# Loading q and k two tokens to a partition, with 64-column transposes, all loads on one queue and a new plan of steps

## The chip, the cores and the metric

The kernel runs on one core of a Trainium2 chip. The metric is the device time of one execution in microseconds (us), and the span of a profile is the part of it from the first to the last instruction. Engines are named as in the profile: PE is TensorE, PEld its weight loads (they overlap PE), DVE is VectorE, ACT is ScalarE, POOL is GpSimd, SP is SyncE. "L476" is a line of the kernel in question, so the same operation has other line numbers in other kernels.

## The reference

It is attention inside chunks of 64 tokens, followed by a layer that mixes tokens and then channels:

```python
# q, k, v: (8 batches, 8 heads, 576 tokens, 64), float32; nine chunks of 64 tokens
scores = (q_c @ k_c.T) / sqrt(64)             # inside each chunk
x = softmax(scores) @ v_c                     # laid out as (8, 576, 512)
theta = x @ w_theta                           # 512 x 512
y = w_tok_r @ (x * cos(theta)) + w_tok_i @ (x * sin(theta))   # 576 x 576, over tokens
u = x + y
out = u + relu(u @ w_ch)                      # 512 x 512, float32
```

## The kernel before

The batches go in four pairs. A pair has 9 blocks of 128 tokens, taken in five groups of two blocks or one (`GROUPS`); the groups of the pair's first half come first (`B0 = [0, 2, 1]`), those of its second half later (`B1 = [3, 4]`). The steps of a group are: a1 transposes q and k (`ps_qkT`), a2 makes the scores (`ps_sT`) and ACT their exponentials (`eT`), a3 multiplies by v (`ps_x`), a4 transposes x (`ps_xT`), and a5 multiplies by theta (`ps_theta`), with cosine and sine on ACT. After them come the token mixing (`ps_y`, with both token weights transposed once at the start into `wT`) and the channel step (`ps_uw`). A small planner, `Order`, keeps estimated clocks of PE, DVE and ACT and decides when the program is built in which order the steps stand. All PSUM results share four slots of 4 KB per partition.

```python
def load_qk(p, j):                       # one block of 128 tokens, one token per partition
    t = nat.tile([P, 2, H, D], FP16, name="qk16")
    nats[p, j] = t
    for ti, ap in enumerate((q, k)):
        for pp, bb, s0, n in in_ranges(j):
            nc.gpsimd.dma_start(t[pp : pp + n, ti],
                ap[2 * p + bb, :, s0 : s0 + n, :].rearrange("h s d -> s h d"))

def a1(p, g):                            # 8 full-size transposes a block, one copy
    ...
                nc.tensor.transpose(psv[:, w, e, jj * P : jj * P + P],
                    t[:, w, 2 * e : 2 * e + 2, :].rearrange("s h d -> s (h d)"), id16)
    ...
    nc.vector.tensor_copy(out=qkT[:, :, :, 0 : n * P], in_=psv[:, :, :, 0 : n * P])

def a2(p, g):                            # 64x64 array tiles, four at a time
    ...
                        nc.tensor.matmul(psv[kh * CH : kh * CH + CH, par, i, e, :],
                            qkT[par * D : par * D + D, 1, e, c0 : c0 + CH],
                            qkT[par * D : par * D + D, 0, e, c0 : c0 + CH])

# the start: weights and the first v as float32 on the hardware queue (SP), cast on chip
tok32 = [load_tok_w(0, moe_w_tok_r), load_tok_w(1, moe_w_tok_i)]
v32 = {0: load_v32(0, 0)}
wth32 = load_w32(moe_w_theta)
new_pair(0)
load_qk(0, 0)                            # q, k: software queue (POOL)
...
# each pair: main steps, and filler steps put between them
od.segment(y0, (front(p, B1) if p == 0 else []) + back(p, B1), tail=3.0)
...
od.segment(mid, fill, tail=4.0)          # mid: y1 and ps_uw by turns; fill: the next pair
# ... (casts, estimates of landing times and the other steps left out)
```

The softmax here doesn't subtract the row's maximum and nothing guards it: scores larger than these inputs give would overflow.

## Time and profile before

| | before |
|---|---|
| time, median of 3 | 243.7 us (242.69 to 245.37) |
| span of the profiled run | 242.2 us |
| first transpose of q | 12.36 us |
| first `ps_y` | 53.14 us |
| from there to the end | 189.1 us |

The prediction below shows the lines of this profile and reads them. One more view belongs here. It cuts the run in two where `ps_y` first starts; its columns are the stretch, its length, then PE, PEld, DVE, ACT and POOL busy (with instructions), the granted clock, the DMA share and GB/s.

```profile
0.00:53.10 53.10, 26.92 (x354) 17.25 (x354) 17.29 (x33) 21.39 (x27) 36.38 (x51) 0.97 1.71 185
53.10:242.20 189.10, 174.11 (x2304) 119.61 (x2288) 113.89 (x188) 91.94 (x112) 71.14 (x93) 0.99 0.97 103
```

PE is empty for 26.2 of the first 53.1 us, and for only 15.0 of the 189.1 after them.

One more row of the page matters later. It gives the clock granted to PE, in tenths, in 40 slices of 6.06 us:

```profile
PEclk9999999889999999999999979999999999999999
```

The 7 is a stretch at half the clock, recorded from 138.82 to 142.24 us: eight `ps_theta` take 3.04 us there and 1.89 us at 98.12. It costs PE some 1.7 us, half of its 3.42. The first seven 9s are not a grant: the trace has no clock record before 43.25 us, and the page prints full clock where there is no record. All 61 full-size matmuls that follow one another without a gap before 43.25 us are spaced for half rate (107 ns for 128 columns).

### The profile page before, as it was taken

To read this page: it belongs to the slowest core of one execution; us is meant where nothing else is said; L and a number is where in the kernel's file an instruction comes from. 1 tells how busy PE (TensorE), PEld (TensorE's weight loads), DVE (VectorE), ACT (ScalarE), POOL (GpSimd) and SP (SyncE) were. 2 spreads that over 40 slices of the span, in tenths; PEclk is the share of its full clock that TensorE was granted. 3 is DMA by queue.
4 is the path that set the end of the run, shared out by engine and by line. 5 is a ranking of instruction groups with operands and counts; after the bars stand their busy time and mean duration, and the time that the engine had idled before them with its cause. 6 is when DMAs were issued, how large, how long until landed. Compare 5 with 4: busy or idle time off the path is not lost.

```text
span 242.2 us, 6094 instructions
## 1 busy us (share of the span) xinstructions
PE 201.0 (83%) x2642; PEld 136.9 (57%) x2642; DVE 131.2 (54%) x220; ACT 113.3 (47%) x138; POOL 107.5 (44%) x143
## 2 busy tenths in 40 slices
PE   0036767589999879999998799999997999998992
PEld 0014554257766756567777555676775556765751
DVE  0103482546546764784567617763866387635453
ACT  2205526662664528823835266536333865361132
POOL 8444776999920019896800097987200100000000
PEclk9999999889999999999999979999999999999999
DMA  6999999999990119999991199999911115100226
GB/s 220 267 194 217 155 157 170 140 132 137 140 80 4 46 46 113 191 226 195 131 62 46 46 106 169 179 232 152 82 46 46 46 56 184 46 0 3 87 96 207
DMA packets 120953, 29.38 MB, mean 121 GB/s; under 512 B 113632, under 2 KB 114656, under 8 KB 120928
## 3 DMA queue, kind: packets, MB, share of 16 engines
q0 software_dynamic: 108048, 14.03, 91.4%
q1 hardware_dynamic: 12880, 14.98, 21.3%
q8 instruction: 20, 0.33, 0.6%
q14 instruction: 5, 0.04, 0.1%
HBM read 33.06 MB, written 9.44 MB: 175 GB/s over the span
## 4 chain that ended last, share of the span: by engine, by line
PE 60%; DVE 5%; ACT 4%; issue 2%; DVEq 0%
PE ps_y L477 25%; PE ps_uw L497 13%; PE ps_theta L421 10%; PE ps_qkT L314 5%; PE ps_uw L504 3%; PE ps_xT L392 2%; DVE uT L485 2%; ACT xT L399 2%; ACT eT L343 1%; PE ps_sT L336 1%; ACT relu L510 1%; DVE x L378 1%; DVE qkT L321 1%; DVE z L444 1%; ACT sin L435 0%
## 5 line engine op out<-in xcount | busy, mean ns | idle before, releaser
L477 PE MATMUL ps_y<-wT,z 128*128 128x288 f16 x512 | 68.5, 286 | 5.5 <-ACT eT L343 2.1
L477 PEld LDWEIGHTS <-z 128*128 128x128 f16 x512 | 48.9, 98 | 19.6 <-issue 3.4
L485 DVE TENSOR_TENSOR uT<-ps_y,xT 128x576 f16<-128x576 f32 x32 | 24.2, 757 | 37.5 <-PE ps_y L477 37.5
L497 PE MATMUL ps_uw<-wch,uT 128*128 128x512 f16 x144 | 41.7, 383 | 1.5 <-ACT xT L399 1.5
L217 POOL DMA_DIRECT2D qk<-in_q_dram x40 | 35.8, 902 | 11.2 <-DMA qk<-in_q_dram 6.9
L236 POOL DMA_DIRECT2D v<-in_v_dram x48 | 36.8, 815 | 7.2 <-DMA qk<-in_k_dram 3.9
L217 POOL DMA_DIRECT2D qk<-in_k_dram x40 | 36.1, 909 | 4.1 <-DMA qk<-in_k_dram 3.0
L314 PE MATMUL ps_qkT<-id,qk 128*128 128x128 f16 x288 | 21.4, 231 | 19.9 <-DMA qk<-in_q_dram 14.5
L421 PE MATMUL ps_theta<-wtheta,xT 128*128 128x512 f16 x128 | 34.0, 418 | 3.7 <-ACT xT L399 3.7
L321 DVE COPY qkT<-ps_qkT 128x2048 f16<-128x2048 f16 (+1 forms) x20 | 21.7, 1114 | 26.0 <-PE ps_qkT L314 26.0
L510 ACT ACTIVATE relu<-ps_uw 128x512 f32<-128x512 f32 x36 | 21.2, 600 | 28.4 <-PE ps_uw L504 28.2
L431 ACT ACTIVATE cos<-ps_theta,pihalf 128x1024 f16<-128x1024 f32 (+1 forms) x20 | 20.6, 1029 | 23.9 <-PE ps_theta L421 21.9
L504 PE MATMUL ps_uw<-id,uT 128*128 128x128 f16 x144 | 31.8, 221 | 0.0
L399 ACT COPY xT<-ps_xT 128x1024 f16<-128x1024 f16 x16 | 15.9, 1015 | 32.1 <-PE ps_xT L392 32.1
L314 PEld LDWEIGHTS <-qk 128*128 128x128 f16 x288 | 17.8, 103 | 22.6 <-DMA qk<-in_q_dram 14.5
L516 DVE TENSOR_TENSOR o<-ps_uw,relu 128x512 f32<-128x512 f32 x36 | 24.1, 688 | 11.0 <-ACT relu L510 10.8
L405 POOL COPY xT<-xTm 128x256 f16<-128x256 f16 x8 | 3.0, 402 | 59.7 <-ACT xTm L403 59.7
L378 DVE TENSOR_TENSOR x<-ps_x,recip 128x512 f16<-128x512 f32 x36 | 24.9, 692 | 1.2
L343 ACT ACTIVATE eT<-ps_sT 128x1024 f16<-128x1024 f32 (+1 forms) x20 | 18.3, 937 | 15.1 <-PE ps_sT L336 15.1
L421 PEld LDWEIGHTS <-xT 128*128 128x128 f16 x128 | 13.1, 106 | 20.3 <-issue 5.1
L497 PEld LDWEIGHTS <-uT 128*128 128x128 f16 x144 | 14.1, 98 | 15.4 <-issue 0.3
L444 DVE TENSOR_TENSOR z<-x,cos 128x1024 f16<-128x1024 f16 x16 | 11.0, 688 | 20.1 <-ACT cos L431 20.0
(41 smaller groups left out, 179.3 us busy)
## 6 DMA issues: line engine op xcount, KB each, us to landing
out_dram<-o SPq DMA_DIRECT2D x32, 256.0 KB, 2.3
qk<-in_q_dram POOLq DMA_DIRECT2D x32, 128.0 KB, 6.0
qk<-in_k_dram POOLq DMA_DIRECT2D x32, 128.0 KB, 6.2
v<-in_v_dram POOLq DMA_DIRECT2D x34, 64.0 KB, 5.5
v<-in_v_dram POOLq DMA_DIRECT2D x14, 128.0 KB, 5.8
wtok<-in_moe_w_tok_r_dram SPq DMA_DIRECT2D x1, 1152.0 KB, 6.0
wtok<-in_moe_w_tok_i_dram SPq DMA_DIRECT2D x1, 1152.0 KB, 10.0
w<-in_moe_w_theta_dram SPq DMA_DIRECT2D x1, 1024.0 KB, 12.9
```

The source lines that it names most:

```text
L217: nc.gpsimd.dma_start(t[pp : pp + n, ti], ap[2 * p + bb, :, s0 : s0 + n, :].rearrange("h s d -> s h d"),)
L236: nc.gpsimd.dma_start(v16[pp : pp + m, sl, :, 0:D], v[2 * p + bb, :, s0 : s0 + m, :].rearrange("h s d -> s h d"),)
L314: nc.tensor.transpose(psv[:, w, e, jj * P : jj * P + P], t[:, w, 2 * e : 2 * e + 2, :].rearrange("s h d -> s (h d)"), id16,)
L321: nc.vector.tensor_copy(out=qkT[:, :, :, 0 : n * P], in_=psv[:, :, :, 0 : n * P])
L378: nc.vector.tensor_tensor(out=xo, in0=px[:, :, :, 0:D], in1=recip.broadcast_to((P, 2, NE, D)), op=ALU.mult,)
L421: nc.tensor.matmul(ps[:, jj * DM : jj * DM + DM], xt[:, db, :], wtheta16[:, db, :], start=(db == 0), stop=(db == NDB - 1),)
L477: nc.tensor.matmul(psv[:, hf, 0:HS], z[:, db * P : db * P + P], wT[:, kt, hf * HS : hf * HS + HS], start=(kt == 0), stop=(kt == 2 * KT),)
L485: nc.vector.tensor_tensor(out=s["uT"][:, db, sl].rearrange("p (f c) -> p f c", f=2), in0=psv[:, :, 0:HS], in1=s["xT"][:, db, sl].rearrange ...
L497: nc.tensor.matmul(ps[:, 0:DM], uT[:, db, j * P : j * P + P], wch16[:, db, :], start=(db == 0), stop=(db == NDB - 1),)
L504: nc.tensor.matmul(ps[:, DM + db * P : DM + db * P + P], uT[:, db, j * P : j * P + P], id16,)
L510: nc.scalar.activation(out=r, in_=ps[:, 0:DM], func=AF.Relu)
L516: nc.vector.tensor_tensor(out=o, in0=ps[:, DM : 2 * DM], in1=r, op=ALU.add)
```

## The change

The intent: with two neighbouring tokens on one partition a run of q or k in memory is 512 B and not 256 B, so q and k need half as many packets. Heads must still come out as 64 rows of features each, so a transpose now takes 64 columns (one head, one token of the two), and two of them fill the array side by side. The q and k copies are split between DVE and ACT, and the k copy puts the tokens back in order. All loads go through the software queue, in the order in which they are used, cast on the way. The planner is changed as well: filler is paced by its heaviest engine, and two `ps_uw` of a pair move into the first stage of the next.

```diff
-    def load_qk(p, j):
-        t = nat.tile([P, 2, H, D], FP16, name="qk16")
+    def load_qk(p, g):
+        j0, n = GROUPS[g]
+        t = nat.tile([P, 2, H, 2, D], FP16, name="qk16")
 ...
-                    t[pp : pp + n, ti],
-                    ap[2 * p + bb, :, s0 : s0 + n, :].rearrange("h s d -> s h d"),
+                    t[(pp // 2) : (pp // 2) + m // 2, ti].rearrange(
+                        "p h t d -> p h (t d)"
+                    ),
+                    src.rearrange("h (p t) d -> p h (t d)", t=2),
 ...  a1
+        for w in range(2):
+            for e in range(NE):
+                for tk in range(2):
+                    for par in range(2):
+                        nc.tensor.transpose(
+                            psv[par * D : par * D + D, w, e, tk, 0:rows],
+                            t[0:rows, w, 2 * e + par, tk, :],
+                            id16[0:rows, 0:rows],
+                        )
+        qT = qkp.tile([P, NE, 2, P], FP16, name="qT")
+        kT = qkp.tile([P, NE, P, 2], FP16, name="kT")
-        nc.vector.tensor_copy(
-            out=qkT[:, :, :, 0 : n * P], in_=psv[:, :, :, 0 : n * P]
+        nc.vector.tensor_copy(out=qT[:, :, :, 0:rows], in_=psv[:, 0, :, :, 0:rows])
+        nc.scalar.copy(
+            out=kT[:, :, 0:rows, :].rearrange("p e s t -> p e t s"),
+            in_=psv[:, 1, :, :, 0:rows],
         )
 ...  a2
+        kT = kT.rearrange("p e s t -> p e (s t)")
+        qT = qT.rearrange("p e t s -> p e s t")
-                            qkT[par * D : par * D + D, 1, e, c0 : c0 + CH],
-                            qkT[par * D : par * D + D, 0, e, c0 : c0 + CH],
+                            kT[par * D : par * D + D, e, c0 : c0 + CH],
+                            qT[par * D : par * D + D, e, c0 // 2 : (c0 + CH) // 2, :],
 ...  the start
-    tok32 = [load_tok_w(0, moe_w_tok_r), load_tok_w(1, moe_w_tok_i)]
-    v32 = {0: load_v32(0, 0)}
-    wth32 = load_w32(moe_w_theta)
     new_pair(0)
-    load_qk(0, 0)
+    load_qk(0, B0[0])
     make_identity(nc, id16)
+    for g in B0[1:]:
+        load_qk(0, g)
+    for g in B0:
+        load_v(0, g)
+    load_w(moe_w_theta, wtheta16)
+    load_tok_w(0, moe_w_tok_r)
+    load_tok_w(1, moe_w_tok_i)
     load_batch(0, B1)
     load_w(moe_w_ch, wch16)
-    (the casts of the float32 weights and of the first v)
 ...  the plan
-        od.segment(y0, (front(p, B1) if p == 0 else []) + back(p, B1), tail=3.0)
+        main = y0[:3] + held[:1] + y0[3:] + held[1:] + ws[0:2]
+        od.segment(main, (front(p, B1) if p == 0 else []) + back(p, B1), tail=4.0)
 ...
+        main = y1[:3] + ws[2:3] + y1[3:] + ws[3:]
+        held = []
+        if more:
+            held = main[-2:]
+            main = main[:-2]
 ...  (planner: pace by the heaviest engine, copies of a step counted side by side)
```

## The prediction

> **What bounds the kernel now.** I read the page's counts first, then its slices, then the table of ten-microsecond stretches, and then the timeline of the stretches that looked wrong.
>
> ```profile
> PE 201.0 (83%) x2642; PEld 136.9 (57%) x2642; DVE 131.2 (54%) x220; ACT 113.3 (47%) x138; POOL 107.5 (44%) x143
> ...
> PE   0036767589999879999998799999997999998992
> ...
> q0 software_dynamic: 108048, 14.03, 91.4%
> ```
>
> TensorE is busy for 201.0 us of 242.2, so 41 us are empty. The PE row says where: the first eight or nine slices (6 us each), a dip at each change of batch pair, and the end. The software DMA queue takes 91.4% of the engines' time, but that share is summed over the run and says nothing yet of who waits. The stretches show it (columns after the length: PE, weight loads, DVE, ACT, POOL busy us and instructions; granted clock; DMA share; GB/s):
>
> ```profile
> 10.00:20.00 10.00, 2.90 (x21) 1.90 (x21) 0.43 (x1) 0.00 (x0) 3.48 (x4) 1.00 1.51 227
> 20.00:30.00 10.00, 7.16 (x96) 5.15 (x96) 4.09 (x8) 6.40 (x9) 6.11 (x9) 1.00 1.98 160
> ...
> 110.00:120.00 10.00, 10.00 (x92) 7.19 (x91) 4.14 (x7) 6.84 (x7) 6.96 (x9) 1.00 2.13 157
> ...
> 180.00:190.00 10.00, 7.87 (x196) 5.45 (x194) 7.17 (x14) 3.99 (x6) 0.74 (x2) 1.00 0.08 28
> ```
>
> From 10 to 20 us the PE works 2.90 us, with ACT and DVE idle as well: all wait for data. From 110 to 120 it is full while the DMA share is 2.13, so in the middle loads are hidden behind TensorE. From 180 to 190 it loses 2.13 us with no DMA to speak of (0.08): there it waits for copies and exponentials at the change of pair. In the sum over ten-microsecond rows, PE is busy 24.25 us of the first 50: 25.75 of the 41 lost us lie there.
>
> The timeline of the start names the waits:
>
> ```profile
> 12.36 0.61 PE L314 MATMUL ps_qkT<-id,qk 128*128 128x128 f16 x4 [12.36 <-DMA qk<-in_q_dram]
> 12.60 0.89 POOL L217 DMA_DIRECT2D qk<-in_q_dram  x1 [4.10 <-DMA qk<-in_q_dram]
> 14.37 0.61 PE L314 MATMUL ps_qkT<-id,qk 128*128 128x128 f16 x4 [1.40 <-DMA qk<-in_k_dram]
> ...
> 32.54 0.83 PE L280 MATMUL ps_wT<-id,wnat 128*64 128x128 f16 x10
> ...
> 39.61 3.60 PE L421 MATMUL ps_theta<-wtheta,xT 128*128 128x512 f16 x8 [0.68 <-ACT xT L399]
> ...
> 53.14 0.66 PE L477 MATMUL ps_y<-wT,z 128*128 128x288 f16 x4
> ```
>
> The first q tile, issued at 1.24 us, lands at 12.36; each following load of 1024 packets lands about 2.1 us after the last, and POOL itself waits (4.10 us): eight loads are out, and the ninth issue reuses the first one's semaphore. The token mixing, the large stage, starts only at 53.14. From there to the end are 189.1 us in which PE hardly stops. So two questions matter: when does ps_y start, and does what follows get longer?
>
> **What the Trainium skill says.** "DMA: Bandwidth & Descriptors", section Specifications, gives 512 B as the smallest transfer at line rate. The packets agree in direction: in the trace a software packet that reads 256 B and writes 128 B holds its engine 32 ns, one that reads 2048 B and writes 1024 B 98 ns, so eight times the bytes for three times the time. The same page, "Queues, rings and completion order", says that an engine takes turns between queues packet by packet. This fits the start: the float32 weights go by the hardware queue in packets of 2304 and 2048 B at 106 and 88 ns, and each 32 ns packet of q waits behind them.
>
> "TensorE: Matmul & The Clock Gate", Part 1, has the array at half rate when little used, and warns that clock records are unreliable. Both show here: eight ps_theta matmuls take 3.60 us at 39.61 and 1.89 us at 98.12, start to start 427 against 216 ns[...]. The tile transposes at 32.54 are in that half-rate time.
>
> "TensorEngine Tiling (Array Packing)", Key Properties, says that tiles load and multiply in parallel and that a change of mode drains the array; its Restrictions say that column tiling loses fast weight load. The transposes of 128x64 at 32.54, just the form that the change uses, start in pairs 3 to 6 ns apart, a pair every 107 ns. Half rate makes 128 columns 107 ns, so a pair costs one full-size transpose and its weight loads stay hidden. The drain shows as well: 125 ns from the last 64x64 matmul to the next full-size one, against 32 ns for a set of four.
>
> **The change, part by part.**
>
> Loads. For q and k two tokens make one run: 512 B read and 256 B written, so 73,728 packets become 36,864. Between the two measured sizes I estimate 41 ns each; the 108,048 packets hold v (32 ns) unchanged. POOL issues 12 loads of q and k per pair, not 20; at 0.9 us for 1024 packets this saves some 8 us of POOL per pair, hidden after the start. What counts is the order: q and k of the first three groups (2.62 MB read), their v (1.31), theta (1.05), then the two token weights (2.65), with no hardware queue beside them. In stretches of 4 us, the start of the kernel before reads at most some 340 GB/s in large packets, and in 256 B packets about 1,100 per us (282 GB/s). With 330 for q and k, 282 for v and 340 for the weights: 7.9 + 4.7 + 3.1 + 7.8 = 23.5 us. Data begins at about 2.6 us (issue at 1.24 and one 1 us issue), and I add 2 us to landing: first q about 6 us, theta about 20, last token weight about 28. The second batch of groups follows until about 38.
>
> Start of ps_y. The nine wT transposes finish last. Five of them need the second token weight; before, a group of this sort took some 0.75 us at half rate, so 3.5 us: ps_y starts at about 31.5 instead of 53.14. Theta and z for the first three groups fit between 20 and 31. Gain: 21.6 us.
>
> Casts. Thirteen casts of v, wnat and wtheta (9.8 us of ACT and DVE together) go; they lie in the waiting time and are worth nothing more than the earlier start.
>
> Work moved behind ps_y. Before, both a1 steps of the second batch and one a2 were done by 53.14 (1.95 and 0.45 us); now they come during ps_y: +2.2 us.
>
> Transposes. A group had 16 of 56 ns (0.89 us); now 16 pairs of about 58 ns (0.93). With one more mode change of about 0.11 us this is +0.15 us a group, 17 groups after the start: +2.5 us. It is on the path, as PE bounds there.
>
> Evacuation. DVE loses a copy of 1221 ns for one of 684 (the 1024-element form), 2.5 us per pair; ACT gains five k copies of about 1015 or 592 ns, 4.7 us per pair. The step gets shorter, 1.22 to about 1.0 us, as both run together. ACT was busy about 26 us per pair of 49, so it can carry this on average.
>
> Order. The last two ps_uw steps of a pair move into the next pair's first stage, the first two into that same stage, and the filler is paced by its heaviest engine, not by PE alone. PE loses 6.25, 5.34 and 3.86 us in gaps over 0.12 us in the three middle periods (half-clock stretches included), most at the change of pair. I give the new order about 1.2 us of each: -3.5.
>
> Sum: -21.6 + 2.2 + 2.5 - 3.5 = -20.4 us; 243.7 - 20.4 = 223.3, say 223 us.
>
> **The rivals.** First, column tiles that expose their weight loads: 64 columns without fast load, 107 ns for a pair at full clock too, would add 0.8 us a group, 14 us over 17 groups: 237 us. The page's restriction speaks for it; the half-rate reading of 32.54 and the 64x64 sets at 32 ns speak against it.
>
> Second, the queue does not get faster. If one queue with at most eight loads out reads at the 212 GB/s of the stretch from 12 to 16 us, 7.63 MB take 36 us, and ps_y begins at about 44: 235 us. Against it: the stretches from 24 to 44 us read 261 to 341 GB/s, and POOL needs only some 16 us to issue it all.
>
> Third, ACT becomes the bound at the change of pair. The y1 stage (second half of a pair, first batch of the next) holds five k copies, five exponentials, five relus, copies, sines and two table loads, by my sum 22.7 us of ACT in about 27 us of PE. If each a1 to a2 step now waits in ACT's queue, 2 to 3 us a pair are lost instead of 1.2 gained: 234 us.
>
> Fourth, the start is better than I think: loads overlap fully, ps_y at 26 us, and the new order removes most gaps: 213 us.
>
> **Range and chances.** The central term, the start of ps_y, I trust to 4 us; the later periods to 2 us each in sum 5. That gives 214 to 232. For less than 2% gain two rivals would have to come true together. Faster by over 2%: 0.95; within 2%: 0.04; slower: 0.01.
>
> **What would show it.** The first transposes at 6 to 8 us, not 12.4; the software queue's share near 70%; ps_y starting at 29 to 34 us; pairs of 128x64 transposes 56 to 60 ns apart at full clock (107 would be rival one); periods of ps_y 47 to 50 us long; in the stretches at the change of pair more than 7.9 of 10 us PE busy, with no new wait for the k copy. A ps_y start after 38 us, or periods longer than 51 us, would make the prediction wrong.

## The result, and the profile after

The changed kernel took 230.23 us (median of 4, 228.72 to 231.85) against 243.19 us (median of 4) for the kernel before in the same rounds. All ratios here are the mean time of one kernel's fast runs over that of the other's from the same rounds, so they are not quite the ratios of the medians: 0.9454, with a 95% interval of 0.9364 to 0.9544. Two later calls of the unchanged kernel gave 0.9582 and 0.9567, so the gain is 4 to 5.5%. The time lies inside the predicted range of 214 to 232 us, 7 us above the predicted 223.

The page of the profiled run (span 226.9 us; this run was the fastest of the four) has these lines for the ones shown of before:

```profile
PE 201.7 (89%) x2994; PEld 140.3 (62%) x2994; DVE 120.2 (53%) x214; ACT 130.5 (58%) x151; POOL 88.5 (39%) x124
...
PE   0678979997898998999898998999898998999992
...
q0 software_dynamic: 77664, 16.54, 82.3%
```

PE's busy time is the same as before, and the span is 15.3 us shorter, so its idle time fell from 41.2 to 25.2 us. The slices at the left, 0036767 before, are now 0678979. The software queue holds 30,384 packets fewer, but its share is only nine points lower, as the weights now come through it. The same ten-microsecond stretches:

```profile
10.00:20.00 10.00, 7.47 (x206) 5.99 (x206) 4.38 (x11) 6.52 (x8) 9.42 (x14) 1.00 1.81 168
20.00:30.00 10.00, 8.76 (x56) 4.79 (x55) 4.29 (x9) 8.02 (x10) 4.49 (x6) 1.00 1.53 186
...
110.00:120.00 10.00, 9.07 (x234) 7.40 (x228) 4.45 (x8) 8.82 (x9) 0.00 (x0) 1.00 0.03 11
180.00:190.00 10.00, 9.21 (x92) 5.33 (x89) 8.03 (x15) 5.75 (x9) 1.02 (x2) 1.00 0.33 96
```

From 10 to 20 us PE now works 7.47 us and not 2.90. The later rows fall in other parts of the work than before, since everything is earlier, so they cannot be compared line by line; the row from 110 is now the change of pair, with ACT busy for 8.82 us of ten. Cut at the first `ps_y`, the run reads:

```profile
0.00:33.50 33.50, 22.24 (x379) 15.62 (x379) 12.27 (x27) 18.70 (x22) 25.57 (x41) 1.00 1.52 156
33.50:226.90 193.40, 179.51 (x2620) 124.70 (x2616) 107.94 (x187) 111.82 (x129) 62.97 (x84) 0.99 0.86 112
```

The first part is 19.6 us shorter. The second is 4.3 us longer: PE is busy 5.4 us more in it and idle 1.1 us less. So in these two profiles the gain is all at the start, and a part is paid back in PE's own work. The timeline of the start:

```profile
5.79 1.07 PE L307 MATMUL ps_qkT<-id,qk 128*64 128x128 f16 x16 [5.79 <-DMA qk<-in_q_dram]
7.47 2.08 PE L307 MATMUL ps_qkT<-id,qk 128*64 128x128 f16 x48 [0.61 <-DMA qk<-in_k_dram]
...
21.38 2.85 PE L420 MATMUL ps_theta<-wtheta,xT 128*128 128x512 f16 x8
27.68 0.87 POOL L225 DMA_DIRECT2D qk<-in_k_dram  x1 [0.93 <-DMA wnat<-in_moe_w_tok_i_dram]
29.34 1.59 PE L271 MATMUL ps_wT<-id,wnat 128*128 128x128 f16 x15 [0.63 <-ACT sin L434]
33.50 2.13 PE L476 MATMUL ps_y<-wT,z 128*128 128x288 f16 x16
```

The first q is there at 5.79 us. POOL's wait at 27.68 ends with the landing of the last token weight. From there `ps_y` is 5.8 us away. The transposes of that weight run at full rate here, but they wait for a PSUM slot that ACT frees late (its sines, at 29.34) and for one that a DVE copy frees (at 31.54), and the last copy of it ends at 33.23. The sines are late in part because the theta step before them ran in part at half rate: eight `ps_theta` at 21.38 take 2.85 us, where 1.9 is the time at full rate. A second profile of the same kernel has 3.48 us for those eight, a recorded half clock from 31.61 us on, and the first `ps_y` at 35.85. This part of the start scatters from run to run.

The step that turns transposes into scores changed most in the middle of the run. In the kernel before, for a group of two blocks:

```profile
122.44 0.45 PE L336 MATMUL ps_sT<-qkT 64*64 64x64 f16 x32
122.81 1.07 PE L314 MATMUL ps_qkT<-id,qk 128*128 128x128 f16 x16
123.92 1.23 DVE L321 COPY qkT<-ps_qkT 128x2048 f16<-128x2048 f16 x1 [0.55 <-PE ps_qkT L314]
```

and in the changed kernel:

```profile
105.05 1.08 PE L307 MATMUL ps_qkT<-id,qk 128*64 128x128 f16 x32
106.39 0.68 DVE L316 COPY qT<-ps_qkT 128x1024 f16<-128x1024 f16 x1
107.11 1.30 ACT L317 COPY kT<-ps_qkT 128x1024 f16<-128x1024 f16 x1 [1.35 <-DVE qT L316]
...
112.80 2.12 PE L476 MATMUL ps_y<-wT,z 128*128 128x288 f16 x16 [0.84 <-ACT eT L342]
...
120.12 0.69 PE L335 MATMUL ps_sT<-qT,kT 64*64 64x64 f16 x32
```

The number after the start is the busy time of the instructions merged in the line. Thirty-two 64-column transposes take what sixteen full-size ones took (1.08 and 1.07 us). The same 32 score matmuls take 0.69 us and not 0.45. The two copies stand one after the other: ACT waits for DVE although they read different halves of the PSUM tile, so the step lasts 0.68 + 1.30 = 1.98 us and not 1.23. And at 112.80 `ps_y` waits for an exponential, which stands on ACT behind a k copy (109.67) and a table load of 1.28 us (110.43). Such a wait is longer here, but not new: in the same period the kernel before has one of 0.69 us at 132.52, and old_layout, below, one of 0.41 us at 120.53.

### The profile page after: what moved, and what is told of

Read it like the earlier page. It is cut to its first block, busy times and chain, and to the rows that moved or that the text cites. A ratio compares the mean times of both kernels' runs of the same rounds, so it can differ in the third digit from the quotient of the medians.

```text
span 226.9 us, 6743 instructions
## 1 busy us (share of the span) xinstructions
PE 201.7 (89%) x2994; PEld 140.3 (62%) x2994; DVE 120.2 (53%) x214; ACT 130.5 (58%) x151; POOL 88.5 (39%) x124
## 3 DMA queue, kind: packets, MB, share of 16 engines
q0 software_dynamic: 77664, 16.54, 82.3%
## 4 chain that ended last, share of the span: by engine, by line
PE 75%; ACT 14%; DVE 6%; DMA 2%; issue 1%; POOL 0%; DVEq 0%; ACTq 0%; POOLq 0%
PE ps_y L476 32%; PE ps_uw L496 13%; PE ps_theta L420 13%; ACT eT L342 5%; PE ps_qkT L307 5%; PE ps_sT L335 3%; PE ps_uw L503 3%; DMA qk<-in_k_dram 2%; PE ps_xT L391 2%; DVE uT L484 2%; DVE x L377 2%; ACT kT L317 2%; ACT cos L430 2%; ACT xT L398 2%; PE ps_x L363 2%
## 5 line engine op out<-in xcount | busy, mean ns | idle before, releaser
L246 POOL DMA_DIRECT2D v<-in_v_dram x56 | 42.1, 776 | 14.6 <-DMA qk<-in_k_dram 9.2
L496 PE MATMUL ps_uw<-wch,uT 128*128 128x512 f16 x144 | 41.0, 379 | 2.3 <-ACT xT L398 1.7
L317 ACT COPY kT<-ps_qkT 128x1024 f16<-128x1024 f16 (+1 forms) x20 | 23.4, 1193 | 17.9 <-DVE qT L316 17.9
L404 POOL COPY xT<-xTm 128x256 f16<-128x256 f16 x8 | 4.9, 652 | 72.3 <-ACT xTm L402 72.3
L420 PE MATMUL ps_theta<-wtheta,xT 128*128 128x512 f16 x128 | 31.2, 388 | 1.7 <-ACT xT L398 1.7
L307 PE MATMUL ps_qkT<-id,qk 128*64 128x128 f16 (+1 forms) x640 | 22.1, 227 | 6.4 <-DMA qk<-in_q_dram 5.8
L307 PEld LDWEIGHTS <-qk 128*64 128x64 f16 (+1 forms) x640 | 18.9, 118 | 9.4 <-DMA qk<-in_q_dram 6.2
L316 DVE COPY qT<-ps_qkT 128x1024 f16<-128x1024 f16 (+1 forms) x20 | 12.6, 636 | 22.7 <-PE ps_qkT L307 22.7
L420 PEld LDWEIGHTS <-xT 128*128 128x128 f16 x128 | 12.6, 100 | 15.7 <-ACT xT L398 2.1
L443 DVE TENSOR_TENSOR z<-x,cos 128x1024 f16<-128x1024 f16 x16 | 11.1, 691 | 20.6 <-ACT cos L430 20.4
L225 POOL DMA_DIRECT2D qk<-in_k_dram x24 | 19.2, 804 | 3.6 <-DMA wch<-in_moe_w_ch_dram 1.6
```

The source lines that it names most:

```text
L246: nc.gpsimd.dma_start(v16[pp : pp + m, sl, :, 0:D], v[2 * p + bb, :, s0 : s0 + m, :].rearrange("h s d -> s h d"),)
L307: nc.tensor.transpose(psv[par * D : par * D + D, w, e, tk, 0:rows], t[0:rows, w, 2 * e + par, tk, :], id16[0:rows, 0:rows],)
L317: nc.scalar.copy(out=kT[:, :, 0:rows, :].rearrange("p e s t -> p e t s"), in_=psv[:, 1, :, :, 0:rows],)
L420: nc.tensor.matmul(ps[:, jj * DM : jj * DM + DM], xt[:, db, :], wtheta16[:, db, :], start=(db == 0), stop=(db == NDB - 1),)
L496: nc.tensor.matmul(ps[:, 0:DM], uT[:, db, j * P : j * P + P], wch16[:, db, :], start=(db == 0), stop=(db == NDB - 1),)
```

## The experiments

Twelve kernels ran; all gave the right result. A period is the time from the first `ps_y` of a pair to that of the next, and the table shows the second one (the first holds most of the scatter of the start). The kernel before took 243.25, 243.01 and 242.17 us in the three calls. Its second period holds the stretch of half clock shown above; its third, which has none, is 48.67 us, so 48.67 is the fairer number to hold against the others: the change's period is 1.9 us longer, and those of old_layout and order_only are the same. The starts and periods are those of one profile each.

| run | median us | ratio to before, 95% | first `ps_y` | second period |
|---|---|---|---|---|
| before | | 1 | 53.14 | 50.36 |
| the change | 230.23 | 0.9454 (0.9364 to 0.9544) | 33.50 | 50.54 |
| **call 1, 3 rounds** | | | | |
| old_layout | 230.76 | 0.9491 (0.9437 to 0.9545) | 38.26 | 48.63 |
| hw_weights | 244.95 | 1.0050 (0.9997 to 1.0103) | 50.29 | 50.55 |
| old_order | 239.81 | 0.9870 (0.9825 to 0.9916) | 36.05 | 51.33 |
| order_only | 242.06 | 0.9952 (0.9902 to 1.0003) | 54.37 | 48.64 |
| **call 2, 5 rounds** | | | | |
| after_again | 232.26 | 0.9582 (0.9523 to 0.9641) | slow profile | slow profile |
| copies_together | 232.23 | 0.9594 (0.9536 to 0.9653) | 33.90 | 50.82 |
| q_interleaved | 233.40 | 0.9643 (0.9602 to 0.9684) | 36.98 | 50.40 |
| q_inter_together | 232.04 | 0.9586 (0.9548 to 0.9624) | 37.26 | 50.98 |
| **call 3, 5 rounds** | | | | |
| after_third | 230.94 | 0.9567 (0.9512 to 0.9622) | 35.85 | 50.54 |
| hybrid | 228.09 | 0.9442 (0.9393 to 0.9490) | 34.04 | 48.87 |
| hybrid_ws | 227.07 | 0.9390 (0.9357 to 0.9424) | 36.94 | 48.08 |
| weights_first | 240.79 | 0.9965 (0.9927 to 1.0002) | 45.74 | 50.54 |

### Which part brings the gain: old_layout, hw_weights, old_order, order_only

My theory was that the gain comes from the early start, that the start comes from the order of the loads on one queue, and that the two-token layout adds little. The rivals were that the layout itself, with its fewer packets, or the new plan brings it.

**old_layout** is the changed kernel with the loads, transposes and the single copy of q and k as before:

```diff
 # against the changed kernel
+    def load_qk1(p, j): ...             # one token per partition, 256 B runs, as before
+    def load_qk(p, g): for j in its blocks: load_qk1(p, j)
 # a1: 8 full-size transposes a block, one DVE copy; a2 reads qkT: as before
```

> The changed kernel with one token per partition again (128x128 transposes, one 1.22 us copy on VectorE, contiguous q), while the single queue in order of use and the new plan of steps stay. Theory (the order of the loads makes the gain, the two-token layout costs after the start): q and k packets fall back to 256 B, ps_y starts 1 to 4 us later than 33.5 (34.5 to 37.5), a set of four score matmuls goes back from 62 to 32 ns, the k copy no longer queues behind the q copy, so the periods shrink from 50.6 to 48 to 49.5; time 226 to 230, not slower than the changed kernel. Rival (the halved packets make the gain): ps_y starts at 40 us or later, time 236 or more.

It took 230.76 us, which can't be told from the change; the first `ps_y` came at 38.26 us. Both lie just above what I expected (226 to 230, and 34.5 to 37.5). These two lines of its timeline name the landing of the last token weight and the first `ps_y`:

```profile
30.72 0.88 POOL L245 DMA_DIRECT2D v<-in_v_dram  x1 [2.28 <-DMA wnat<-in_moe_w_tok_i_dram]
...
38.26 2.13 PE L467 MATMUL ps_y<-wT,z 128*128 128x288 f16 x8
```

The weight lands 3.0 us later than in the change (3.7 later than in its second profile), so the larger packets do help the start. But each later period is 1.9 us shorter than the change's, and that gives the start's gain back. As a whole the layout is worth nothing here.

**hw_weights** puts float32 weights and the first v back on the hardware queue, with their casts:

```diff
 # against the changed kernel
-        nc.gpsimd.dma_start(wnat[ri]..., ...)     # theta and the first v likewise
+        f32 = pairp.tile([P, KT + 1, S], FP32, name="wtok32", tag="uT")
+        nc.sync.dma_start(f32..., ...)            # and the casts of before
```

> The changed kernel with the float32 weights and the first v on the hardware queue and cast on VectorE and ScalarE again, two-token layout kept. Theory (order makes the gain): the first q lands at 9 to 12 us instead of 5.8, ps_y starts at 42 to 50 us, time 238 to 246. Rival (halved packets make the gain, order does not matter): ps_y before 38 us, time 234 or less.

At 244.95 us the whole gain is gone. The start of its timeline shows why:

```profile
13.09 1.06 PE L326 MATMUL ps_qkT<-id,qk 128*64 128x128 f16 x16 [13.09 <-DMA qk<-in_q_dram]
```

The first q lands at 13.09 us, although its load is issued first on its own queue and has the large packets; the first `ps_y` starts at 50.29 us. Both are a little past what I expected (9 to 12, and 42 to 50). The packets of the trace show two parts in the delay of q. Its first packet starts at 5.94 us here (5.83 in the kernel before) and at 2.96 in the change, though the load is issued at 1.24 us in all three. From 7.2 to 10 us the two queues then take turns, 369 packets of q and k to 354 of the weights (381 to 380 in the kernel before). What holds the first packet back for 3 us no run shows. The larger packets alone, next to a second queue, bring 4.1 us of start against order_only (54.37), and the longer periods take them back.

**old_order** is the change with the plan of before:

```diff
 # against the changed kernel
-        work = sum(s.load for s in filler)
+        work = sum(s.pe for s in filler)
-        main = y0[:3] + held[:1] + y0[3:] + held[1:] + ws[0:2]
-        od.segment(main, ...)
+        od.segment(y0, ...)
+        mid: y1 and ps_uw by turns, nothing held over        # and the old clock in Order.do
```

> The changed kernel with the plan of steps of the kernel before (sequence of ps_y and ps_uw, pacing by TensorE alone, copies planned one after the other). Theory (the new plan gains little): ps_y starts within 1 us of 33.5 and what follows takes 192 to 196 us instead of 193.4, time 228 to 233. Rival (the plan is what keeps ScalarE's new work off the path): what follows takes 198 us or more, time 235 or more.

This one went against me: 239.81 us. The start is early (36.05), but the first period takes 62.48 us where the change has 53.22. With an early start the second batch of the first pair comes in the first `ps_y` stage, and that stage had only four `ps_y` steps to cover it. The two lines of old_order are an ACT table load, a part of the delay, and the wait of PE:

```profile
52.08 1.28 ACT L429 ACT_TABLE_LOAD   x1 [3.53 <-PE ps_theta L419]
...
56.35 3.47 PE L419 MATMUL ps_theta<-wtheta,xT 128*128 128x512 f16 x8 [3.91 <-ACT xT L397]
```

In the changed kernel the same wait is

```profile
52.34 1.90 PE L420 MATMUL ps_theta<-wtheta,xT 128*128 128x512 f16 x8 [1.74 <-ACT xT L398]
```

because two `ps_uw` steps stand in front of it. PE in old_order waits 3.91 us for the copy of x (behind the table load, a cosine and a sine), and then the eight matmuls run at half rate, 3.47 us and not 1.90. These two items are 3.7 us of the 9.3. A second stretch of half clock, from 76.63 to 80.04 us, adds some 1.7; the rest is spread over the period and I have not followed it.

**order_only** is the other side of that: the kernel before with the new plan alone.

```diff
 # against the kernel before
-        work = sum(s.pe for s in filler)
+        work = sum(s.load for s in filler)
-        od.segment(y0, ...)
+        main = y0[:3] + held[:1] + y0[3:] + held[1:] + ws[0:2]
+        od.segment(main, ...)
+        main = y1[:3] + ws[2:3] + y1[3:] + ws[3:]    # its last two held for the next pair
 # the loads, the casts, a1 and a2 stay as before (the identity is made one block's loads later)
```

> The new plan of steps alone: loads, casts and one-token layout of the kernel before. Theory: ps_y starts near 53 us as before, the periods lose 1 us each at most; time 240 to 244 against 243.2. Rival (the plan is worth several us by itself, and the layout ate it): time 238 or less.

It took 242.06 us, 1.2 us under the kernel before, and its interval reaches 1. So the plan is worth about one microsecond with the old loads. Its second period is 1.7 us shorter than that of the kernel before, as long as the stretch of half clock costs there, and its third is the same (48.63 and 48.67). With the early loads the plan is worth 7 to 10: the ratio of 0.987 without it against 0.945 to 0.958 for the change, times 243. The two parts interact: here the plan is the condition for keeping what the loads bring. As old_order has the two-token layout too, and no run has the early loads with the old layout and the old plan, the share of the layout in this is not separated; the first period of old_order is 9.3 us longer than the change's, the later ones 0.8.

### What makes a period longer: after_again, copies_together, q_interleaved, q_inter_together

The two-token layout costs 1.9 us a period. I had two suspects from the traces: the k copy, which follows the q copy and delays an exponential (0.84 us of idle PE before the `ps_y` at 112.80 in the record, 1.03 us measured from start to start), and the score matmuls, which read q in steps of two tokens.

**after_again** is the changed kernel once more, as a base.

> The changed kernel unedited, as the measure for the other runs of this call: 0.9454 of the kernel before, within 0.009; periods 50.5 to 50.6 us.

Its profiled execution fell in the slow state (271.13 us at a granted clock of 0.77), so only its timed fast runs count: 230.22 to 233.23 us. Their ratio of 0.9582 lies above the 0.9544 that I had allowed, so the size of the gain itself differs between calls.

**copies_together** gives q and k a PSUM tile each, so that the two copies have no tile in common:

```diff
 # against the changed kernel
-        ps = psum2("ps_qkT", FP16)
-        psv = ps.rearrange("p (w e t s) -> p w e t s", w=2, e=NE, t=2)
+        psv = [psum2(f"ps_{c}T", FP16).rearrange(
+                   "p (x e t s) -> p x e t s", x=2, e=NE, t=2)[:, 0] for c in "qk"]
```

> q and k transposed into two PSUM tiles, so that the k copy no longer waits for the q copy; the plan of steps stays, each group now holds two of the four PSUM slots for a while. Theory (the copies one after the other stretch the step from transposes to scores to 2.0 us, and PE waits for it at the change of pair): the k copy starts with the q copy, the 1.03 us gap before ps_y at the change of pair falls to 0.4 or less, periods 49.6 to 50.2, time 1 to 3 us under the changed kernel. Rival (the wait is hidden, or the slots bind instead): periods 50.4 or more, time within 1 us of the changed kernel or above it.

The copies do run together now:

```profile
108.86 1.30 ACT L320 COPY kT<-ps_kT 128x1024 f16<-128x1024 f16 x1 [0.42 <-PE ps_kT L310]
109.08 0.68 DVE L319 COPY qT<-ps_qT 128x1024 f16<-128x1024 f16 x1
```

ACT waits for PE alone. So what made it wait before was that the two reads shared one tile, which the program builder put in order; the engines themselves can read two PSUM tiles at once (both copies run from 109.08 to 109.76). The idle time of 1.03 us before `ps_y` is gone too. But the period is 50.82 us, no shorter, and the time is that of after_again (232.23 and 232.26 us), as the rival said: a group now takes two of the four PSUM slots, and PE waits 0.84 us a period, start to start, between the transposes of q and those of k, until an exponential has read a slot (at 114.92). So the run does not decide the theory that this wait is what a period loses: it was replaced by another wait of nearly the same size.

**q_interleaved** makes the q copy write the tokens in order, as the k copy does, so that the score matmuls read q without steps:

```diff
 # against the changed kernel
-        qT = qkp.tile([P, NE, 2, P], FP16, name="qT")
-        nc.vector.tensor_copy(out=qT[:, :, :, 0:rows], in_=...)
+        qT = qkp.tile([P, NE, P, 2], FP16, name="qT")
+        nc.vector.tensor_copy(out=qT[:, :, 0:rows, :].rearrange("p e s t -> p e t s"), in_=...)
 # a2
-                            qT[par * D : par * D + D, e, c0 // 2 : (c0 + CH) // 2, :],
+                            qT[par * D : par * D + D, e, c0 : c0 + CH],
```

> The q copy writes tokens in order (a step of two elements, as the k copy does), so that the score matmuls read q contiguously. Theory (the read in steps is what halves their rate): a set of four goes from 62 to about 32 ns, PE saves about 1.1 us a period; the q copy on VectorE grows from 0.69 to 0.9 to 1.3 us and the k copy behind it starts as much later; periods 49.3 to 50.3. Rival (the mix of tile modes or the weight loads slow them): sets stay at 55 ns or more, periods 50.6 or more.

A set of four score matmuls fell from 62 to 32 ns, the time of the kernel before. That settles the cause of the slow scores: it is the stepped read, and not a change of array mode, which is the same in both. But the period fell by 0.14 us only, not to 49.3 to 50.3, and the time did not fall (233.40 us, against 232.26). The groups of instructions (busy us, mean ns, then idle before them and its end) of q_interleaved, and below those of the change, show what took its place:

```profile
L316 DVE COPY qT<-ps_qkT 128x1024 f16<-128x1024 f16 x16 | 20.7, 1300 | 20.7 <-PE ps_qkT L307 20.7
```

```profile
L317 ACT COPY kT<-ps_qkT 128x1024 f16<-128x1024 f16 x16 | 20.7, 1306 | 15.4 <-DVE qT L316 15.4
...
L316 DVE COPY qT<-ps_qkT 128x1024 f16<-128x1024 f16 x16 | 11.0, 690 | 22.4 <-PE ps_qkT L307 22.4
```

Writing 2-byte elements in steps of two costs DVE 1300 ns and not 690, and the k copy of 1306 ns still stands behind it. The pair then takes 2.6 us.

**q_inter_together** joins the two edits, so that both copies of 1.3 us run side by side.

> Both edits. Theory: what the two-token layout costs after the start (1.93 us a period against the old layout) is the score matmuls and the serial copies, so the periods come back to 48.4 to 49.4, time 3 to 6 us under the changed kernel. Rival (mode changes and ScalarE's load hold the rest): periods 49.8 or more.

I expected a period of 48.4 to 49.4 us and got 50.98. In that period PE waits before transposes of q (0.67 us), before those of k (0.37) and before a `ps_y` (0.73), start to start, each time until DVE or ACT has done with a tile. I did not separate which reader costs how much. The layout has its price in several places, and the kernel turns each repair into a wait at another.

### A version between the two, and a control for the queue: after_third, hybrid, hybrid_ws, weights_first

**after_third** is the changed kernel, as the base.

> The changed kernel unedited, as the measure for this call: ratio 0.945 to 0.959 to the kernel before.

Its profile is the second one quoted above: first `ps_y` at 35.85 us, periods of 50.54 and 50.55.

**hybrid** uses the two-token layout for the first pair only, where its packets shorten the start, and the old one for the other three pairs:

```diff
 # against the changed kernel
+    def load_qk(p, g):
+        return (load_qk1 if p else load_qk2)(p, g)
+    def a1(p, g):
+        return (a1_one if p else a1_two)(p, g)       # and a2 reads what the pair has
```

> Two tokens per partition for the first batch pair only; pairs two to four use one token, full-size transposes, one copy on VectorE. Queue, order of loads and plan of steps as changed. Theory (the two-token layout gains only at the start, 4.8 us of it, and costs 1.9 us a period later): ps_y starts at 33.5 to 34.5, periods 48.5 to 49, time 3 to 5 us under the changed kernel of the same call, ratio about 0.94. Rival (the doubled q and k packets of later pairs are not hidden once the start is early, or the first period swallows the gain): periods 50 or more, time within 1.5 us of the changed kernel.

It took 228.09 us, 2.85 us under after_third, a little less than the 3 to 5 that I expected. The start stays early (34.04) and the second period is 48.87 us.

**hybrid_ws** adds one more thing: of the first pair, four `ps_uw` steps and not two stand behind the first `ps_y` stage, to fill the wait of 1.9 us that the change still has there.

```diff
 # against hybrid
+        ne = 2 if p else 4
-        main = y0[:3] + held[:1] + y0[3:] + held[1:] + ws[0:2]
+        main = y0[:3] + held[:1] + y0[3:] + held[1:] + ws[0:ne]
-        main = y1[:3] + ws[2:3] + y1[3:] + ws[3:]
+        main = y1[:3] + (ws[2:3] if p else []) + y1[3:] + ws[3 if p else 4:]
```

> The same, with four instead of two ps_uw steps of the first pair put behind its first ps_y stage, where TensorE waits 1.9 us for the copy of xT. Theory: that gap goes, but the next stage has 2.2 us less work to cover its copies, so 0 to 1.5 us under the run before it. Rival: the next stage loses as much, no difference or slower.

It took 227.07 us, the fastest of all: 6.1% under the kernel before by the ratio of the same rounds. The step from hybrid is inside the scatter of the two, so I claim only that both hybrids beat the change. In its profile (229.02 us, the slowest of its seven runs) the wait of 1.9 us is gone, but one of 1.0 us stands before a `ps_uw`, and the first period is 53.79 us against 52.74 in hybrid.

**weights_first** keeps all loads on the one software queue, but puts the three weights at its head:

```diff
 # against the changed kernel
+    load_tok_w(0, moe_w_tok_r)
+    load_tok_w(1, moe_w_tok_i)
+    load_w(moe_w_theta, wtheta16)
     new_pair(0)
     load_qk(0, B0[0])
 ...
-    (the same three loads after v)
```

> The changed kernel with theta and both token weights at the head of the single queue instead of behind the first v. Theory (position in the queue is what counts, as all loads share one rate of some 330 GB/s): the first q lands near 14 to 16 us, the last of the first v near 28, so the whole chain from transposes to z of the first groups follows after it and ps_y starts at 38 to 44 us, time 5 to 9 us over the changed kernel. Rival (only the second queue was the trouble; order within one queue does not matter): ps_y at 33 to 35.5 us, time within 2 us of the changed kernel.

```profile
15.43 1.06 PE L307 MATMUL ps_qkT<-id,qk 128*64 128x128 f16 x16 [15.43 <-DMA qk<-in_q_dram]
...
45.74 2.37 PE L476 MATMUL ps_y<-wT,z 128*128 128x288 f16 x16
```

At 240.79 us nearly the whole gain is lost, with one queue and no hardware queue beside it. The first `ps_y` came at 45.74 us, later than the 38 to 44 that I expected, and the time is 9.9 us over after_third, where I expected 5 to 9. So the gain is not that of a single queue as such: it is that q and k come before the weights, and the hardware queue of the kernel before was one way of letting the weights come in ahead. It is not the whole difference, though: hw_weights starts `ps_y` another 4.6 us later, although its first q lands 2.3 us earlier, and its ratio is 0.0085 higher, some 2 us. Whether its casts on chip or the second queue cost that, no run separates.

One cause could not be tried. Full-size transposes of the two-token tile would need a stationary operand with two free dimensions, and leaving k in steps for the scores would need the same; the program builder refuses both (the stationary operand must have exactly one free dimension). That is why the change has 64-column tiles and puts k back in order.

## Why the prediction was right or wrong, point by point

I divide PE's time between the first `ps_y` and the last matmul by start-to-start distances: what exceeds the streaming time of a matmul by over 0.1 us counts as a gap, the rest as streaming. This makes each term of the predicted sum measurable. The predicted -20.4 us became -15.3 us between the spans of the two profiles (242.2 and 226.9 us); the terms, read from the traces, add up to within 0.2 us of that. The split between gaps and streaming depends on the threshold by a few tenths of a microsecond.

| term of the prediction | predicted us | measured us |
|---|---|---|
| start of `ps_y` | -21.6 | -19.6 (second profile -17.3) |
| work moved behind it | +2.2 | +1.2 |
| transposes | +2.5 | +2.5 |
| order, fewer gaps | -3.5 | -3.0 |
| reads of q by the scores | none | +3.4 |
| other lines together | none | +0.4 |
| sum | -20.4 | -15.1 |

**Loads: right, but for the queue's share.** I had estimated 41 ns for a packet that reads 512 B, and it measures 41. First q at 5.79 us (predicted about 6), last token weight at 27.68 and 27.01 in the two profiles (predicted about 28). Rival two, a queue that gets no faster, is refuted. The share "near 70%" was wrong: it is 82.3%, because I had not counted the weights and the first v that move onto this queue.

**Start of ps_y: right cause, 2 to 4 us too early.** The step "a group of this sort took some 0.75 us at half rate, so 3.5 us" failed in size: it took 5.8 us, and 8.8 in the second profile. I had counted the transposes and not their wait for PSUM slots held up by ACT's sines, nor the half rate that comes and goes in the theta steps before. The second profile also lies outside the 29 to 34 us that I had named as a sign. What brings the start is shown by the factorial, one profile for each corner and two for the change: one queue in order instead of two (and no casts on chip) brings 16.1 us with the old layout (54.37 to 38.26) and 14.4 to 16.8 us with the new one (50.29 to 35.85 or 33.50); weights_first shows that position counts with one queue alone. The larger packets bring the other 2.4 to 4.8 us.

**Work moved: over-estimated.** One of the two a1 steps that I moved had still been done before `ps_y` (32 transposes at 32.48 us), so only one a1 (0.94 us) and one a2 (0.27) came behind it.

**Transposes: right.** A pair of 128x64 comes every 56 ns at full rate, so rival one (107 ns) is refuted. Streaming grew by 0.1 us beyond the moved group. The gaps of 0.03 to 0.2 us next to transposes went from 5 with 0.6 us in all to 24 with 3.0 us. The sum is +2.5, but not all of it belongs to the 64-column form: old_layout has 16 such gaps with 1.7 us, as the new plan alternates transposes and scores more often.

**Evacuation: wrong.** "The step gets shorter, 1.22 to about 1.0 us, as both run together" failed twice. They do not run together, since both copies read one PSUM tile and the builder orders them. And the k copy takes 1306 ns where I had put the 1015 of a plain ACT copy. It writes in steps of two, which is probably why: for the q copy on DVE q_interleaved shows that (690 to 1300 ns), for ACT no run takes the step away. The step is 2.0 us. What I had named as a sign of failure, "no new wait for the k copy", came: 15.4 us of ACT's idle time end with the q copy, and the exponential after it holds `ps_y` up by 1.03 us a period, where the kernel before loses 0.85 us before one `ps_y` of this stage and old_layout 0.57 (start to start). copies_together shows that the order comes from the shared tile, but also that its removal alone gains nothing.

**Reads of q: the missed term.** I never asked how the scores would read q, which now lies with its two tokens 256 B apart. A set of four 64x64 matmuls takes 62 ns and not 32. q_interleaved brings it back to 32 by the layout alone, so this is shown. By the set times (36 sets a period, 30 ns each) it is about half of what the layout adds to a period, 1.0 of the 1.9 us; gaps are the other 0.9 (4.9 us a period against 4.0 in old_layout).

**Order: nearly right in size, for a reason not seen.** Leaving out the small gaps next to transposes, gaps fell by 3.0 us (17.7 to 14.8). But some 1.6 us of this is the half-rate matmuls at 138.82 to 142.24 us in the kernel before, which count as gaps in this method, so that the size came out near -3.5 is in part luck. None of the eleven fast profiles with the new plan has a half clock in its second or third period, and one of the two with the old plan has; that is too few to say that the plan prevents it. But order_only and old_order show that this term does not stand alone: the plan is worth about 1 us with late loads and 7 to 10 with early ones. In the sum I treated the start and the order as two additive terms. Without the new plan the first `ps_y` stage would have had to absorb the second batch, and most of the start's gain would have gone there.

**Rival three**, ACT as the bound at the change of pair, was the nearest to the truth in kind: ACT is busy 8.82 of 10 us there and delays `ps_y`. With a smaller one at 117.82, the waits before `ps_y` in this stage are 1.3 us a period (start to start), against 0.85 in the kernel before and 0.57 in old_layout: 0.4 to 0.7 us more, and not 2 to 3. **Rival four** did not occur.

**Signs.** The periods were to be 47 to 50 us long and are 53.22, 50.54 and 50.55; the first is past the 51 us that I had named as making the prediction wrong. By that sign of its own this part of the account failed, though the time stayed in the range.

The result stayed in the range, but 7 us above the predicted time, because its two large errors have the same sign: a start 2 to 4 us later and 3.4 us of slower scores. The scatter of the start does the rest, as the profiled run (228.72 us) was the fastest of four.

## What to carry to other kernels

At a start that waits for data, first ask in which order the bytes arrive over all queues; a second queue lets its bytes in ahead of what is needed first, and so does a bad position in a single queue. When a layout is changed for the sake of a load, follow the tile to its last reader, since copies that write in steps and matmuls that read in steps can cost in each period what the load saved once; a mixed version, with the layout only where the load is on the path, can then beat both. And an earlier start changes what stands beside the first heavy stage, so the order of steps must be made again with it.

## What the Trainium skill lacked or had wrong

- "Advanced Engine Details and Errata", section SBUF Cachelines, says that accesses that each hit a different 16-byte line are penalised. I overlooked it in the prediction. The runs agree in direction, without testing the line size, and give a cost that it lacks: four 64x64 matmuls take 62 ns with the moving q read in elements 256 B apart, and 32 ns with them adjacent.
- "DMA: Bandwidth & Descriptors", section Issuing engines are not separate DMA queues, says that several issuing engines only save issue time. It does not say what a second queue can cost: float32 weights on the hardware queue put the first q off from 5.79 to 13.09 us and the first `ps_y` from 33.5 (or 35.9) to 50.29 us. Weights at the head of one queue did the same in kind (15.43 and 45.74 us).
- No page that I found has packet times of loads that cast from float32 to 16 bits. Here a packet that reads 256, 512, 2048 or 2304 B held its engine 32, 41, 98 or 107 ns.
- "TensorEngine Tiling (Array Packing)", section Restrictions, says that column tiling switches fast weight load off. No cost of it shows here: a pair of 128x64 transposes comes every 56 ns, the time of one full-size transpose.
- No page that I found gives the cost of an ACT copy whose output goes in steps of two 2-byte elements: 1306 ns for 1024 elements a partition, against some 1015 ns for a plain one.
